# Attention decode over four layers on one core: more TensorE loops, sums folded into the heads' product, one maximum product, wo rows in two banks

## The chip, the core and the metric

The kernel runs on one core of a Trainium2 chip. The metric is the device time of one execution in microseconds (us). The engines named below are TensorE (PE, with its weight loads shown as PEld), VectorE (DVE), ScalarE (ACT), GpSimd (POOL) and SyncE (SP), which issues nearly all transfers.

## What is computed

Four layers of one-token attention over a cache, A, B, A, B, each with 32 heads of 192 numbers and 8192 cached keys and values per head. All tensors are bf16; x has 640 numbers.

```python
def _A_ref(x, k_cache, v_cache, wq, wo):
    ...
    q = (x @ wq).reshape(B, Sq, Hq, Dh).transpose(0, 2, 1, 3)
    ...
    scores = jnp.einsum("bhqd,bhkd->bhqk", q, k) * (Dh ** -0.5)
    p = _softmax(scores, axis=-1)
    o = jnp.einsum("bhqk,bhkd->bhqd", p, v)
    return o.transpose(0, 2, 1, 3).reshape(B, Sq, Hq * Dh) @ wo
...
x = A_x
x = x + _A_ref(_layernorm(x, axis=-1), A_k_cache, A_v_cache, A_wq, A_wo)
x = x + _B_ref(_layernorm(x, axis=-1), B_k_cache, B_v_cache, B_wq, B_wo)
x = x + _A_ref(_layernorm(x, axis=-1), A_k_cache, A_v_cache, A_wq, A_wo)
x = x + _B_ref(_layernorm(x, axis=-1), B_k_cache, B_v_cache, B_wq, B_wo)
```

_B_ref computes the same as _A_ref. The caches do not fit on the core, so nearly all of them is read twice.

## The kernel before

**Tiling.** Heads are taken two at a time: 16 pairs in each of 4 layers. A pair's keys lie on 128 partitions, 64 for each head, 128 keys per partition, and are handled in two halves u = 0, 1 of 64 keys (3072 KB each); so are its values. They land in `pool`, eight slots of one half each. A whole pair of keys or values is one transfer of 6144 KB into two slots, or two of 3072 KB (`whole`).

**Order.** Python lists fix the order. `steps` is the order of compute, `plan` that of the transfers; `allot` gives each transfer the slots that come free first, `released` says after which step, and `transfer` lets SP wait for the event in `freed`. SP has one queue in order: a transfer that waits for its slot holds up all behind it. Each engine's instructions are a `Queue`; `settle` drops waits that others imply, and `bank` makes users of one PSUM bank wait for the last use by other engines.

**Steps of a pair.** For pair p of layer l, `products` (step m, L693) multiplies each half of the keys by q on VectorE in place (L705), in NC cuts over the 192 numbers: two cuts of 96 in pairs 2 to 13 of layers 0, 1 and 3, four of 48 elsewhere. TensorE sums over the numbers with the identity as weights, 24 products a half of 8 numbers x 64 keys into `S`: in pairs with two cuts by `matmul_loop` (L83, a loop on TensorE with two products a turn, L95) apart from the first and last two, else written out (L725). Layer 2's pair 0 goes in quarters (`quarter`). `softmax` (step s) reduces S to scores (L785), takes the largest of each partition (L787), brings these across the partitions by two products of 64 columns (L790), reduces them to the negated maximum (L794), and lets ScalarE form the exponentials and their sums (L800). `values` (step v) sums the sums of exponentials over the partitions (L815, or L819 for the last pair) into bank TB and multiplies the exponentials with the values into O in bank group OY, in four column groups (L842), eight keys at a time, or two in a layer's last pair. `gather` (step e) takes the reciprocal of the sums (L856), picks the wanted parts of O on VectorE (L866 and L868, or L861 and L862 for the last pair), sums them by the heads' product into TB (L880, or L876), and scales them into `rows` by ScalarE (L889).

**Steps of a layer.** `q_rows` and `q_spread` (L606) form the row of all q and spread the pair's part over the partitions into bank QM (L610, copied at L572); q_spread for the next pair stands behind the second half's scores. After pairs 4, 9 and 14, `columns` (L681) turns the gathered row into columns and `project_row` (L651) multiplies 15 of them with the block of wo: for each column, two products of 320 numbers (L658) into YR, partitions 0 and 32 of one bank. `to_columns` turns the row sum into columns (L671, L675); in layer 1 that follows the second block, and the third is done in columns by `project` (L624). In layers 1 and 3 the last 5 and 7 columns of the third block are a transfer and a step of their own (wob), and the last value half comes in two quarters (vq). `busy` gives TensorE products without use to keep its clock up.

**The end.** In layer 3 the last steps are: m of pair 15, v of pair 14, s of 15, busy 16, e of 14, first half of v of 15, columns, eight columns of wo, second half of v of 15 with busy 6 ahead of its last quarter, e of 15 with busy 3, and ten columns of wo (7 in wob, 2 in wol, 1 in woe). ScalarE copies YR (L948) and SP sends it out.

Of the kernel before, what the change touches and what calls it, by code (L numbers as in the profile page):

```python
# [5 lines left out]
ALU = mybir.AluOpType  # L6
# [76 lines left out]
def matmul_loop(t, waits, out, lhsT, rows, first, count, regs, at, label, begin):  # L83

    b, width, m = t.bass, out.shape[-1] // rows.shape[1], len(regs)
    for i in range(m if begin else 0):
        t.reg_mov(regs[i], at + 2 * (first + i * width))
# [19 lines left out]
NSLOT = 8  # L107
KEPT = {0: {("k", 0)}, 1: {("v", 14), ("v", 15)}}


def build(nc, A_x, A_k, A_v, A_wq, A_wo, B_x, B_k, B_v, B_wq, B_wo, out):
# [28 lines left out]
    with ExitStack() as ctx:  # L140
# [19 lines left out]
        acc = sb("acc", [P, DH], F32)  # L160
        q_sb = [sb(f"q_sb{i}", [P, DH], BF16) for i in range(2)]
        ones = sb("ones", [P, 1], F32)
        one_b = sb("one_b", [P, 1], BF16)
        small = sb("small", [P, 82], F32)
# [7 lines left out]
        half = col(2)  # L172
        half33 = col(33)
        neghalf = col(1)
        s_sb = [sb(f"s_sb{i}", [P, J], F32) for i in range(2)]
# [3 lines left out]
        l_col = [col(2) for i in range(2)]  # L179
# [12 lines left out]
        zero = sb("zero", [P, 33], BF16)  # L192
        part = [sb(f"part{i}", [P, DC], BF16) for i in range(3)]
# [8 lines left out]
        YR = YB[0:33, 64:64 + HD]  # L202
        TB = ps("TB")
        use = {b: {} for b in ("QM", "S0", "S1", "O", "TB", "YB")}
        QMu, Ou, TBu, YBu = [(use[b],) for b in ("QM", "O", "TB", "YB")]
# [3 lines left out]
        C_ST = 64  # L209
        C_L = 72  # L210
        C_O = 128
# [15 lines left out]
        PO.op(lambda g: g.memset(zero[:], 0.0))  # L227
        mask = acc[:, 0:2 * VK].rearrange("p (h i) -> p h i", h=2)
# [9 lines left out]
        PO.op(lambda g: g.memset(half33, 0.0))  # L238
        ev_const = PO.op(lambda g: g.memset(neghalf[:], -0.5))
        DV.op(lambda v: v.tensor_reduce(pick[:], mask.rearrange("p h i -> p i h"), AX.X, ALU.add), ev_mask)  # L240
        e = DV.op(lambda v: v.tensor_reduce(half[:], mask, AX.X, ALU.add), ev_mask)
        ev_pick = DV.op(lambda v: v.tensor_copy(half33[:, 0:33:32], half[:]), e, ev_const)
# [273 lines left out]
        def sums(ev_z):  # L516
# [5 lines left out]
            e = PE.op(lambda t: t.matmul(TB[:, C_ST:C_ST + 2], lhsT=ones[:, 0:1].broadcast_to([P, P]), rhs=st[:], start=True, stop=True),  # L522
                      e, ev_const, last["stt"], bank=TBu)
            last["st"] = e
            e = DV.op(lambda v: v.tensor_scalar(mv[:], TB[:, C_ST:C_ST + 2], 1.0 / D, None, ALU.mult), e, last["rs"], bank=TBu)
# [3 lines left out]
        def layer(l, ev_z, ev_true):  # L529
# [76 lines left out]
            def q_spread(p):  # L606

                PE.wait(last["rows"], last["QB"], ev_const)
# [22 lines left out]

            def to_row():

                e = DV.op(lambda v: v.tensor_copy(z[:], x_true[:]), ev_true)
                for i in range(3):
                    e = DV.op(lambda v, i=i: v.tensor_copy(part[i][:], z[:]), e)
                    if i < 2:
                        e = DV.op(lambda v, i=i: v.tensor_tensor(z[:], z[:], part[i][:], ALU.subtract), e)
# [373 lines left out]
```

## Time and profile before

| what | value |
|---|---|
| median of 3 runs | 1980.01 us (1979.34 to 1980.67) |
| the profiled execution | 1979.76 us, of which the span is 1978.0 |
| PE, PEld busy | 1272.5 us, 129.3 us |
| DVE, ACT busy | 1198.5 us, 168.1 us |
| mean granted TensorE clock | 0.788 |
| read from HBM | 848.36 MB, 429 GB/s over the span |
| L705, products of keys and q | 837.5 us in 360 instructions |
| L95 and L77 into S, looped and held score products | 382.3 us in 1440, 426.1 us in 1564 |
| L658, wo rows | 41.1 us in 330 |

The span runs from the first to the last instruction, the time of an execution also holds what lies around it. A matmul's end is modelled, so intervals between starts say more of TensorE than its busy time. The granted clock is the share of full speed that the throttle lets TensorE have; the trace has it at 0.50 or 1.00 for some microseconds each.

### The profile page before, as it was taken

To read this page: it belongs to the slowest core of one execution; us is meant where nothing else is said; L and a number is where in the kernel's file an instruction comes from. 1 tells how busy PE (TensorE), PEld (TensorE's weight loads), DVE (VectorE), ACT (ScalarE), POOL (GpSimd) and SP (SyncE) were. 2 spreads that over 40 slices of the span, in tenths; PEclk is the share of its full clock that TensorE was granted. 3 is DMA by queue.
4 is the path that set the end of the run, shared out by engine and by line. 5 is a ranking of instruction groups with operands and counts; after the bars stand their busy time and mean duration, and the time that the engine had idled before them with its cause. 6 is when DMAs were issued, how large, how long until landed. Compare 5 with 4: busy or idle time off the path is not lost.

```text
span 1978.0 us, 13592 instructions
## 1 busy us (share of the span) xinstructions
PE 1272.5 (64%) x7742; PEld 129.3 (7%) x2599; DVE 1198.5 (61%) x812; ACT 168.1 (8%) x529; POOL 4.6 (0%) x24
## 2 busy tenths in 40 slices
PE   3566566567465666665775665666676667657558
PEld 0000000000200100000020000000002001000001
DVE  3566466467166656656755565665764665765756
ACT  0000000000000100100010000000000100000000
POOL 0000000000000000000000000000000000000000
PEclk9787777777687777787887877878787787878778
DMA  9999999999999999999999999999999999999998
GB/s 414 435 434 430 433 431 431 436 432 427 433 436 434 432 430 430 430 431 433 429 415 435 426 426 433 431 430 431 434 429 428 434 431 434 432 432 434 432 432 373
DMA packets 27093, 849.09 MB, mean 429 GB/s; under 512 B 3106, under 2 KB 3236, under 8 KB 3876
## 3 DMA queue, kind: packets, MB, share of 16 engines
q1 hardware_dynamic: 26900, 848.38, 99.7%
q8 instruction: 38, 0.62, 0.1%
q14 instruction: 11, 0.09, 0.0%
q10 hardware_dynamic: 144, 0.00, 0.0%
HBM read 848.36 MB, written 0.00 MB: 429 GB/s over the span
## 4 chain that ended last, share of the span: by engine, by line
DMA 53%; PE 29%; DVE 16%; ACT 2%; issue 1%; SPq 0%
DMA pool<-in_B_k_cache_dram 22%; DMA pool<-in_A_v_cache_dram 15%; DMA pool<-in_A_k_cache_dram 14%; DVE pool L705 11%; PE S L95 8%; PE S L77 7%; PE OY L77 5%; PE OY L842 4%; DMA pool<-in_B_v_cache_dram 2%; DVE s_sb L785 2%; PE OY L658 1%; DVE OY L866 1%; DVE acc L868 1%; ACT p_sb L800 1%; PE S L725 0%
## 5 line engine op out<-in xcount | busy, mean ns | idle before, releaser
L705 DVE TENSOR_TENSOR pool<-pool,q_sb 128x3072 bf16<-128x3072 bf16 (+1 forms) x360 | 837.5, 2392 | 147.0 <-DMA pool<-in_B_k_cache_dram 81.9
L77 PE MATMUL S<-pool,ident 128*128 128x512 bf16 x1564 | 426.1, 422 | 10.8 <-DVE pool L705 10.3
L95 PE MATMUL S<-pool,ident 128*128 x1440 | 382.3, 427 | 2.5 <-DVE pool L705 2.3
L866 DVE TENSOR_TENSOR OY<-OY,small 128x1536 f32<-128x1536 f32 x60 | 106.0, 1766 | 254.2 <-PE OY L77 254.1
L77 PE MATMUL OY<-pool,p_sb 128*16 128x512 bf16 x1920 | 206.2, 518 | 0.0
L880 PE MATMUL TB<-acc,small 128*33 128x192 f32 x120 | 44.5, 467 | 210.3 <-DVE acc L868 210.3
L785 DVE TENSOR_REDUCE s_sb<-S 128x128 f32<-128x1024 f32 x63 | 77.1, 1224 | 163.3 <-PE S L77 163.3
L842 PE MATMUL OY<-pool,p_sb 128*16 128x512 bf16 (+1 forms) x1216 | 144.2, 497 | 47.5 <-DMA pool<-in_A_v_cache_dram 43.9
L725 PE MATMUL S<-pool,ident 128*128 128x512 bf16 x36 | 21.0, 584 | 153.4 <-DVE pool L705 153.4
L572 ACT ACTIVATE q_sb<-QM 64x192 bf16<-64x192 f32 x120 | 38.9, 324 | 941.5 <-PE QM L610 940.8
L868 DVE TENSOR_REDUCE acc<-OY 128x192 f32<-128x1536 f32 x60 | 105.4, 1757 | 2.0
L889 ACT ACTIVATE rows<-TB,small 1x192 bf16<-1x192 f32 x120 | 49.4, 412 | 556.2 <-PE TB L880 554.7
L800 ACT ACTIVATE p_sb<-s_sb,small 64x128 bf16<-64x128 f32 x128 | 55.7, 435 | 170.1 <-DVE small L794 169.3
L856 DVE RECIPROCAL small<-TB 33x2 f32<-33x2 f32 x64 | 11.1, 173 | 95.0 <-PE TB L815 78.2
L790 PE MATMUL QM<-ident,m_bf 128*64 128x64 bf16 x128 | 14.1, 217 | 82.5 <-DVE m_bf L787 82.5
L815 PE MATMUL TB<-small,ones 128*33 128x2 f32 x120 | 14.5, 191 | 74.0 <-ACT p_sb L800 74.0
L742 PE MATMUL S<-pool,ident 128*128 128x512 bf16 x28 | 15.8, 563 | 58.7 <-DVE pool L705 58.7
L610 PEld LDWEIGHTS QM<-rows,one_b 1*128 1x128 bf16 x60 | 5.5, 91 | 734.4 <-issue 728.5
L842 PEld LDWEIGHTS OY<-pool,p_sb 128*16 128x16 bf16 (+1 forms) x1216 | 35.6, 108 | 199.1 <-issue 141.5
L658 PE MATMUL OY<-pool,oT 128*1 128x320 bf16 x330 | 41.1, 431 | 2.2 <-ACT oT L688 2.2
L794 DVE TENSOR_REDUCE small<-QM 128x1 f32<-128x64 f32 x64 | 14.3, 224 | 29.9 <-PE QM L790 29.9
L880 PEld LDWEIGHTS TB<-acc,small 128*33 128x33 f32 x120 | 10.1, 130 | 294.9 <-DVE acc L868 289.7
(90 smaller groups left out, 279.3 us busy)
## 6 DMA issues: line engine op xcount, KB each, us to landing
pool<-in_B_k_cache_dram SPq DMA_DIRECT2D x28, 6144.0 KB, 35.9
pool<-in_B_v_cache_dram SPq DMA_DIRECT2D x28, 6144.0 KB, 29.2
pool<-in_A_v_cache_dram SPq DMA_DIRECT2D x27, 6144.0 KB, 26.3
pool<-in_A_k_cache_dram SPq DMA_DIRECT2D x34, 3072.0 KB, 20.4
pool<-in_A_k_cache_dram SPq DMA_DIRECT2D x14, 6144.0 KB, 34.5
pool<-in_A_v_cache_dram SPq DMA_DIRECT2D x9, 3072.0 KB, 14.5
pool<-in_B_k_cache_dram SPq DMA_DIRECT2D x8, 3072.0 KB, 21.4
pool<-in_A_wo_dram SPq DMA_DIRECT2D x6, 2400.0 KB, 21.2
```

The costliest lines, as they stand in the source:

```text
L77: return t.add_instruction(mybir.InstMatmult(name=t.bass.get_next_instruction_name(), engine=mybir.EngineType.PE, ins=[t.lower_ap(rhs), t. ...
L95: t.add_instruction(mybir.InstMatmult(name=b.get_next_instruction_name(), engine=mybir.EngineType.PE, ins=[x.__replace__(regref=reg.name, ...
L572: lambda a, h=h, r=r, f=f: a.activation(q_sb[i][r, :], QM[r, h * DH:(h + 1) * DH], ACT.Copy, scale=f),
L658: e = PE.op(lambda t, i=i, h=h, f=l < 3 and n[2] == 0 and i == 0, fin=n == last_row and i == k - 1: t.matmul(YR[32 * h:32 * h + 1, :], lhs ...
L705: e = DV.op(lambda v, d0=d0: v.tensor_tensor(k3[:, :, d0:d0 + QD], kin[:, :, d0:d0 + QD], q_sb[qi][:, d0:d0 + QD].unsqueeze(1).broadcast_t ...
L785: lambda v: v.tensor_reduce(s[:], S_[:].rearrange("p (j r) -> p j r", r=R), AX.X, ALU.add),
L800: ev_p[p] = AC.op(lambda a, h=h, r=r: a.activation(p_sb[par][r, :, h], s[r, :], ACT.Exp, bias=negm[par][r, 0:1], accum_out=l_col[par][r, h ...
L842: t.matmul(o, lhsT=x, rhs=y, start=f, stop=fin) if c == 0 else
L866: e = DV.op(lambda v: v.tensor_tensor(o3, o3, pick[:, 0:VK].unsqueeze(2).broadcast_to([P, VK, DH]), ALU.mult), bank=Ou)
L868: e = DV.op(lambda v: v.tensor_reduce(acc[:], O.rearrange("p (i d) -> p d i", d=DH), AX.X, ALU.add), e, bank=Ou)
L880: e = PE.op(lambda t: t.matmul(TB[64:97, C_O:C_O + DH], lhsT=half33, rhs=acc[:], start=True, stop=True), bank=TBu)
L889: last["TO"] = last["row_written"] = AC.op(lambda a, h=h: a.activation(orow[:, o0 + h * DH:o0 + (h + 1) * DH], TB[64 + 32 * h:65 + 32 * h, ...
```

## The change

Eight edits, in one diff:

- **Cuts and loops.** Every half of keys is cut in two, and both halves of its score products run as loops. The pairs of layer and number in `FINE` are cut in 96, 48 and 48, with a loop for the first cut alone. Registers for the loops are set by an addition.
- **Sums of exponentials.** They lie beside `acc` in one tile, and the heads' product takes both: weights `heads` (ones in columns 0 to 32, the heads' masks at 64 and 96), two more moving columns. L815 is gone but for a layer's last pair. The reciprocal and the row copies, `rest`, are put off to the next call of `finish`.
- **Maximum.** One product of 128 columns; the negated maximum is reduced in two halves of the partitions.
- **Wo rows.** The two products of a column go to partition 0 of two banks, YB and YC, the second with the first one's weights. The row's copy is two instructions, one on ScalarE and one on VectorE.
- **Banks.** TB's uses move to QM; its place is YC.
- **Layer 1's third wo block** is done in rows, and `to_columns` follows it, not the second.
- **Layer 0's last pair** takes eight keys at a time, as other pairs do.
- **q_spread** for the next pair stands behind the first half's scores, and the last score product of the second half waits for the copied q.

```diff
-        t.reg_mov(regs[i], at + 2 * (first + i * width))
+        t.reg_add(regs[i], t.zero_reg, at + 2 * (first + i * width))
...
+FINE = {(1, 15), (2, 1), (2, 15), (3, 0)}
...
+        acc_l = sb("acc", [P, DH + 4], F32)
+        acc = acc_l[:, 2:2 + DH]
...
+        heads = col(97)
+        half = heads[:, 64:97:32]
...
+        l_col = [acc_l[:, i * (DH + 2):i * (DH + 2) + 2] for i in range(2)]
...
-        YR = YB[0:33, 64:64 + HD]
-        TB = ps("TB")
+        YC = ps("YC")
+        YR = [b[0:1, 64:64 + HD] for b in (YB, YC)]
...
             def q_spread(p):
 
+                finish()
                 PE.wait(last["rows"], last["QB"], ev_const)
...
+            def pair_of_rows(x, rhs, start, stop, signal):
+
+                for h in range(2):
+                    e = PE.op(lambda t, h=h: (matmul_held(t, YR[1], x, rhs(1), start, stop, 32, 0) if h else
+                                              t.matmul(YR[0], lhsT=x, rhs=rhs(0), start=start, stop=stop, skip_group_check=True)),
+                              signal=signal and h == 1, bank=YRu[h])
+                return e
...
-            last_row = ("woe", l) if l == 3 else ("wo", l, 1 if NB[l] else 2)
+            last_row = ("woe", l) if l == 3 else ("wo", l, 2)
...
-                    for h in range(2):
-                        e = PE.op(lambda t, i=i, h=h, f=l < 3 and n[2] == 0 and i == 0, fin=n == last_row and i == k - 1: t.matmul(
-                            YR[32 * h:32 * h + 1, :], lhsT=o[:, i:i + 1], rhs=t3[:, i, h * HD:(h + 1) * HD], start=f, stop=fin,
-                            skip_group_check=True), signal=(i == k - 1 and h == 1), bank=YBu)
-                last["oT"] = e
+                    e = pair_of_rows(o[:, i:i + 1], lambda h, i=i: t3[:, i, h * HD:(h + 1) * HD],
+                                     l < 3 and n[2] == 0 and i == 0, n == last_row and i == k - 1, i == k - 1)
+                last["oT"] = freed[("woa",) + n[1:]] = e
...
+            def row_copies(a, ev_y):
+
+                return (AC.op(lambda c: c.activation(a[0:1], YR[0], ACT.Copy), ev_y, bank=YBu),
+                        DV.op(lambda v: v.tensor_copy(a[32:33], YR[1]), ev_y, bank=YCu))
...
+            end_keys = VK if l == 0 else 2
+            undone = []
+
+            def finish():
+                if undone:
+                    undone.pop()()
...
-                NC = 2 if l != 2 and 2 <= p < NPAIR - 2 else 4
-                QD = DH // NC
-                for c in range(NC):
-                    d0 = c * QD
-                    e = DV.op(lambda v, d0=d0: v.tensor_tensor(
+                cuts = [DH // 2] + [DH // 4] * 2 if (l, p) in FINE else [DH // 2] * 2
+                starts = [sum(cuts[:c]) for c in range(len(cuts))]
+                for d0, QD in zip(starts, cuts):
+                    e = DV.op(lambda v, d0=d0, QD=QD: v.tensor_tensor(
...
+                    finish()
...
+                        if u == 1 and r == DH // R - 1:
+                            PE.wait(ev_q.get(p + 1))
...
+                PE.wait(chunks[0])
+                scores(0, m)
+                loop(0)
+                PE.wait(chunks[1])
+                if len(cuts) == 2:
+                    loop(1)
+                    e = scores(DH // R - m, DH // R)
+                else:
+                    scores(n, n + n // 2)
+                    PE.wait(chunks[2])
+                    e = scores(n + n // 2, DH // R)
...
+                e = PE.op(lambda t: t.matmul(QM[:, C_MX:C_MX + P], lhsT=m[:, 0:1].broadcast_to([P, P]), rhs=ident[:],
+                                             start=True, stop=True), ev_m, last["MX"], bank=QMu)
+                last["m"][par] = e
                 for h in range(2):
...
+                    r = slice(64 * h, 64 * h + 64)
+                    ev_n = DV.op(lambda v, r=r: v.tensor_reduce(negm[par][r], QM[r, C_MX + r.start:C_MX + r.stop], AX.X, ALU.max,
+                                                                negate=True), e, last["negm"][par], signal=h == 1, bank=QMu)
...
+                x = acc_l[:, 2 * par:2 * par + DH + 2]
+                cl, co = (DH, 0) if par else (0, 2)
+                last["acc"] = last["lc"][par] = e = PE.op(lambda t: t.matmul(
+                    QM[0:97, 0:DH + 2], lhsT=heads, rhs=x, start=True, stop=True), ev_p[p], bank=QMu)
+
+                def rest():
+                    ev_rl = last["rl"] = DV.op(lambda v: v.reciprocal(rl[64:97, 0:2], QM[0:33, cl:cl + 2]), e, last["TO"], bank=QMu)
...
+                undone.append(rest)
...
-                if q_ready and (n[0] in ("wq", "r") and l >= 2 or n[0] == "m" and n[3] == 1):
+                if q_ready and (n[0] in ("wq", "r") and l >= 2 or n[0] == "m" and n[3] == 0):
```

## The prediction, made before the change was run

> **What bounds the kernel now.** I read the page's queue part first, then the slices, then the chain of waits at its end, then the engines' timeline there.
>
> ```profile
> DMA  9999999999999999999999999999999999999998
> ...
> q1 hardware_dynamic: 26900, 848.38, 99.7%
> ```
>
> The cache queue holds the 16 DMA engines 99.7% of the span and no slice shows a hole: 848 MB are read as fast as they come, whatever the engines do. So inside the span an engine's gain is worth nothing, and its loss nothing while the queue keeps a transfer in hand. What counts lies behind the landing of the last key pair but one at 1924.4. The chain of waits (start, length, what) has that transfer last and compute alone behind it:
>
> ```profile
> 1882.28 42.12 DMA pool<-in_B_k_cache_dram
> ...
> 1924.42 1.77 DVE pool L705
> ...
> 1968.05 0.98 PE OY L658 x12
> ...
> 1970.27 1.08 PE S L77 x5
> ```
>
> The timeline gives its durations (start, length, engine, line, and in brackets the idle time before):
>
> ```profile
> 1924.42 13.44 DVE L705 TENSOR_TENSOR pool<-pool,q_sb 128x3072 bf16<-128x3072 bf16 x8 [1.32 <-DMA pool<-in_B_k_cache_dram]
> ...
> 1939.50 1.22 DVE L785 TENSOR_REDUCE s_sb<-S 128x128 f32<-128x1024 f32 x1 [1.64 <-PE S L77]
> ...
> 1941.36 0.23 DVE L794 TENSOR_REDUCE small<-QM 128x1 f32<-128x64 f32 x1 [0.32 <-PE QM L790]
> 1941.50 13.43 DVE L705 TENSOR_TENSOR pool<-pool,q_sb 128x3072 bf16<-128x3072 bf16 x8
> ...
> 1956.56 1.22 DVE L785 TENSOR_REDUCE s_sb<-S 128x128 f32<-128x1024 f32 x1 [1.63 <-PE S L77]
> ...
> 1959.83 0.17 DVE L856 RECIPROCAL small<-TB 33x2 f32<-33x2 f32 x1
> ...
> 1960.03 1.77 DVE L866 TENSOR_TENSOR OY<-OY,small 128x1536 f32<-128x1536 f32 x1
> ...
> 1971.29 0.82 PE L842 MATMUL OY<-pool,p_sb 128*4 128x384 bf16 x16
> ...
> 1973.95 1.11 PE L658 MATMUL OY<-pool,oT 128*1 128x320 bf16 x14
> ```
>
> L705 of pair 14, S, softmax, L705 of pair 15, S, the values of pair 14, L866 and L868, heads, columns, wo rows, the last quarter of the values, wo rows, copy, output: each starts where the one before ends. In it PE meets the last value transfer: the fifth filler product on L77 starts at 1970.97 and the values restart at 1971.29, where the transfer landed at 1971.25. At a filler's 0.216 us PE would have been free at 1971.19, so its slack there is 0.1 us. The tail is both the only place where the change can cost, and a place with no cover.
>
> **The change, part by part.** The profiled execution took 1979.76 us, span 1978.0; the median of the runs shown is 1980.01, 0.25 more.
>
> *Score cuts.* Pairs 0, 1, 14, 15 and layer 2 had four cuts a half; now all have two, but for the four in FINE, with three. Layer 3's pairs 14 and 15 are not in FINE. Two-cut pairs of layer 3 read so in the same view:
>
> ```profile
> 1789.43 1.22 DVE L785 TENSOR_REDUCE s_sb<-S 128x128 f32<-128x1024 f32 x1 [3.38 <-PE S L77]
> ...
> 1866.29 13.16 DVE L705 TENSOR_TENSOR pool<-pool,q_sb 128x6144 bf16<-128x6144 bf16 x4 [1.24 <-DMA pool<-in_B_k_cache_dram]
> 1882.29 1.23 DVE L785 TENSOR_REDUCE s_sb<-S 128x128 f32<-128x1024 f32 x1 [2.84 <-PE S L77]
> ...
> 1912.11 1.22 DVE L785 TENSOR_REDUCE s_sb<-S 128x128 f32<-128x1024 f32 x1 [3.59 <-PE S L77]
> ```
>
> VectorE needs 13.16 instead of 13.44 and 13.43: -0.55 over both pairs. But twelve products wait for the last cut, not six, and the idle time before L785 is 2.84 five times and 3.38, 3.64, 3.59 in the last eight two-cut pairs, mean 3.10 (the long ones where the granted clock was still 0.50 well into the pair), against 1.64 and 1.63 here. That is 2 x (3.10 - 1.635) = +2.93; bounds +2.41 (2.84 twice) and +4.01 (3.64 twice).
>
> *Maximum.* One product of 128 columns replaces two of 64 (L790, 0.22 together): 0. The reduction L794 becomes two of half the partitions, 0.23 each, by the row: +0.25 after pair 14, with its 0.02 hop. After pair 15 it takes the place of the reciprocal L856 (0.20 with its hop), which moves: +0.05. Bounds: 0 if a half costs half, 0.5.
>
> *Sums in the heads' product.* L815 (0.16 on the chain, 1956.53 to 1956.68) goes: -0.16. The heads' product gets 97 weight columns instead of 33 and 194 moving columns instead of 192; L880 took 0.53 for its two passes, a load of 64 columns (L819) 0.13 instead of 0.11: +0.05. The reciprocal now follows this product, and the two L889 copies follow it: +0.20 (0.17 and a hop). For pair 13 the deferred reciprocal slips in between L705's first cut and the second of pair 14: +0.20. Sum +0.29; bounds 0 and 0.5.
>
> *Wo rows.* Each row's two products went to PSUM partitions 0 and 32; now both go to partition 0, in two banks, with one weight load. At granted clock 1.0, single starts on L658 in the tail stand in twos, 2 to 4 ns apart, and 135 ns from pair to pair: 320 columns are streamed once for both. Products on one position stand apart by their full stream: 216 ns for 512 columns on L77, so 135 for 320. A row then takes 270 instead of 135, and the saved load, which PEld runs beside the products, gives nothing back. Eight rows before the wait: +1.08, less the 0.10 of slack; ten after it: +1.35. Bounds: 0 if two banks overlap, +2.43.
>
> The Trainium skill ("TensorE: Matmul & The Clock Gate", section "Why this matters for your kernels") says that small-M matmuls run at once when their outputs lie in different column groups of partitions, and puts three such at 2.38 times, not 3. Taken as 79% of the ideal, an estimate from that page, two would gain 1.59 and the rows would lose 18 x 80 ns = 1.4 instead of 2.43, the whole sum being 1.0 lower. The trace's 2 to 4 ns between starts speaks for the full factor, so I keep 2.43.
>
> *Copy at the end.* L948 (0.43 for 33 partitions) becomes one row on ScalarE and one on VectorE, side by side; L889 takes 0.41 for one row: 0.
>
> *Loops.* They save PE instructions. The instruction queue holds 0.1% of 16 engines: 38 fetches of 16 KB, about 1.05 us of one engine each, so 40/16 = 2.5 us of the stream in all. About 20 score instructions in each of 23 pairs, the 165 second loads of rows, and L815 are roughly 900 of the 10,341 that the page counts on PE and PEld: 9% of 2.5, -0.2, as the stream reaches 1924.4 that much sooner. Bounds 0 and -0.5.
>
> *Under cover.* The same edits delay earlier stages: a wo block there runs mostly at clock 0.50, 267 ns a row (L658, 1173.74 to 1177.70), so +2.0 to +3.7 each; the score end +1.3; in layer 0 the last pair's gather takes L866 and L868 (3.5) instead of L861 and L862 (0.9), +2.6; in layer 1 to_columns (L671, L675, 2.5) moves from the second wo block behind the third, and L624's columns become rows: about +4, less 1.6 that PE idles for the value landing at 1008.78. All of this delays slot releases and so SP's next transfers, which queue in order behind one wait. The cover is the transfer still in flight: between issue and the landing ahead of it lie mostly 8 to 25 us, least 4.2 (value half issued at 1177.74, behind a wo block, landing ahead 1181.94), then 4.5 (1054.47), 5.4 (1328.34) and 5.5 (852.85, 1542.60). The first transfer needed 1.0 from issue to its first packet. Worst: 4.2 - 2.3 = 1.9, still over 1.0. Cost 0; without cover 1 to 3 us at each. The q product moves from behind the second half's scores to behind the first half's; it issues no transfer and passes no DMA queue, and the new wait for q before the last score product, with the maximum and the values queued behind it, ends about 6 us early. The uses of TB move into QM's bank and wait on one another; those on the chain are counted above.
>
> *Sum.* -0.55 + 2.93 + 0.25 + 0.05 - 0.16 + 0.05 + 0.20 + 0.20 + 1.08 - 0.10 + 1.35 - 0.20 = +5.1. 1979.76 + 5.1 + 0.25 = **1985.1 us**, +0.26%. One cannot tell less than 0.2%, about 4 us, from no change here. With the bounds of scores and rows alone it runs from 1982.2 to 1986.2.
>
> **Rivals.**
> (1) The queue runs dry: if the wo blocks after 1173 and 1324 stay at clock 0.50 throughout (+3.7) and the score end adds its 1.3, the 4.2 and 5.4 go under 1.0 and the stream loses 1 to 2 us at each: 1988. For: these blocks start at 0.50. Against: the clock goes to 1.00 at 1177.37 and 1327.55, and v's release there does not wait for scores.
> (2) Other side: the two rows overlap though on one position, since they write two banks. Then the 2.43 falls out: 1982.7, within 0.2%, not slower. It decides once a row takes under about 200 ns at clock 1.0. For: nothing but the two banks. Against: L77's 216 ns, held weights.
> (3) The wider cuts do not delay the end of S (PE warm throughout): 1985.1 - 2.9 = 1982.2. Against: all eight rows.
> (4) The loops free the stream by more than I think: even all fetches gone are 2.5, against 5.3 lost. Faster only if most of the tail's costs fall too.
>
> **How the numbers follow.** Forecast 0.66, (1) 0.12, (2) 0.12, (3) 0.05, (4) 0.05. Slower by over 0.2%: (1), and of the forecast all but its low end: 0.70. Same: that end 0.08, (2), (3): 0.25. Faster: 0.05. The range reaches from (2) and (3), 1982.0, to (1), 1988.5.
>
> **What would show it.** The key landing before pair 14 still near 1924; idle before the S reductions of pairs 14 and 15 near 3 instead of 1.6; rows 270 ns apart in the tail and the last ten taking 2.7 instead of 1.4; PE, no longer the landing, setting the restart of the last values, near 1975. A DMA share under 0.9 in some slice between 1050 and 1560 would show (1); row starts 135 apart (2). I am wrong if the landing near 1924 moves by over 2 us, or the span from it to the end does not grow.

## The result, and the profile after

| | before | changed |
|---|---|---|
| median (lowest to highest, runs) | 1980.03 us (1979.28 to 1980.67, 6) | 1994.9 us (1990.64 to 1999.18, 6) |
| ratio, with its 95% interval | | 1.0075 (1.0062 to 1.0088) |
| the profiled execution | 1979.76 us, span 1978.0 | 1999.18 us, span 1997.4 |
| landing of the key pair ahead of pair 14, layer 3 | 1924.40 | 1934.92 |
| from that landing to the issue of the output | 51.57 | 60.47 |

The change makes the kernel 14.9 us slower by the medians; 5.1 was predicted. The last two rows split the difference of the profiled executions: the stream arrives 10.52 later and the tail takes 8.90 more, together 19.42, which is 1999.18 - 1979.76. The profiled execution is the longest of the six, so this split is that of a long one; the profile of e14_fill3, further down, the same instructions up to the tail, splits into 7.64 and 6.33.

The rates of the kernel before by slice, then of the changed kernel the slices of the DMA engines and of the rate, and its cache queue:

```profile
GB/s 414 435 434 430 433 431 431 436 432 427 433 436 434 432 430 430 430 431 433 429 415 435 426 426 433 431 430 431 434 429 428 434 431 434 432 432 434 432 432 373
```

```profile
DMA  9999999999999999999999999999999999999997
GB/s 412 434 432 433 428 437 429 436 429 427 435 436 429 435 429 434 432 430 435 416 371 413 430 414 439 425 412 433 432 433 425 434 430 437 436 423 435 437 428 304
...
q1 hardware_dynamic: 26900, 848.38, 99.0%
```

The digits hide what the rates show: the 21st slice (999 to 1048 us) moved 371 GB/s, where the kernel before moved 415. The views by window, first of the kernel before, then of the changed one (window, length, busy time of PE, PEld, DVE, ACT and POOL, granted clock, share of the DMA engines, GB/s):

```profile
1020.00:1030.00 10.00, 9.77 (x59) 0.46 (x9) 10.00 (x8) 0.00 (x0) 0.00 (x0) 1.00 0.99 402
1180.00:1190.00 10.00, 8.58 (x38) 0.00 (x0) 8.20 (x5) 0.00 (x0) 0.00 (x0) 1.00 1.01 433
1340.00:1350.00 10.00, 6.72 (x61) 0.83 (x21) 2.53 (x6) 1.63 (x6) 0.00 (x0) 0.83 1.00 430
1962.43:1965.85 3.42, 1.93 (x26) 0.69 (x26) 1.16 (x1) 0.82 (x2) 0.00 (x0) 1.00 1.00 424
```

```profile
1020.00:1030.00 10.00, 7.98 (x59) 2.28 (x35) 5.80 (x13) 0.83 (x2) 0.55 (x1) 0.83 0.78 278
1180.00:1190.00 10.00, 9.21 (x57) 2.61 (x31) 6.96 (x3) 0.62 (x3) 0.00 (x0) 0.75 0.88 351
1340.00:1350.00 10.00, 9.57 (x48) 0.53 (x6) 9.08 (x3) 0.65 (x2) 0.00 (x0) 1.00 0.82 327
1976.79:1980.21 3.42, 1.60 (x23) 0.83 (x26) 1.13 (x3) 0.83 (x2) 0.00 (x0) 1.00 1.01 426
```

In the first three windows the DMA engines stood idle for 2.2, 1.2 and 1.8 us where before they were full: the hand-over from layer 1 to layer 2, and the places behind the first two wo blocks of layer 2. There the queue runs dry. Idle time is not all of it: from 975 to 1075 us the share is 0.95 where it was 1.00, and the rate 385 GB/s where it was 420. Of some 8 us of stream lost in these 100, about 5 are idle time; in the rest the engines are busy and move less, and why no run shows. The fourth line of each belongs to the tail and is read below.

The timeline of the tail in the changed kernel (start, length, engine, line, and in brackets the idle time before):

```profile
1934.95 3.36 DVE L727 TENSOR_TENSOR pool<-pool,q_sb 128x6144 bf16<-128x6144 bf16 x1 [1.30 <-DMA pool<-in_B_k_cache_dram]
...
1938.53 9.90 DVE L727 TENSOR_TENSOR pool<-pool,q_sb 128x6144 bf16<-128x6144 bf16 x3
...
1951.41 1.23 DVE L805 TENSOR_REDUCE s_sb<-S 128x128 f32<-128x1024 f32 x1 [2.99 <-PE S L77]
...
1953.28 0.46 DVE L814 TENSOR_REDUCE small<-QM 64x1 f32<-64x64 f32 x2 [0.32 <-PE QM L809]
...
1970.68 1.23 DVE L805 TENSOR_REDUCE s_sb<-S 128x128 f32<-128x1024 f32 x1 [3.75 <-PE S L77]
...
1979.35 0.28 PE L836 MATMUL QM<-acc,small 128*64 128x1 f32 x4 [1.14 <-ACT rows L912]
...
1979.56 2.15 PE L860 MATMUL OY<-pool,p_sb 128*4 128x384 bf16 x32
...
1983.47 0.47 PE L642 MATMUL OY<-pool,oT 128*1 128x320 bf16 x1
1983.73 0.47 PE L77 MATMUL YC<-pool,oT 128*1 128x320 bf16 x1
...
1984.00 0.47 PE L642 MATMUL OY<-pool,oT 128*1 128x320 bf16 x1
...
1989.27 0.82 PE L860 MATMUL OY<-pool,p_sb 128*4 128x384 bf16 x16
...
1992.44 0.30 PE L642 MATMUL OY<-pool,oT 128*1 128x320 bf16 x1
1992.58 0.30 PE L77 MATMUL YC<-pool,oT 128*1 128x320 bf16 x1
...
1992.71 0.30 PE L642 MATMUL OY<-pool,oT 128*1 128x320 bf16 x1
...
1994.81 0.43 ACT L682 ACTIVATE pool<-OY 1x320 bf16<-1x320 f32 x1 [2.54 <-PE YC L77]
1994.81 0.48 DVE L683 CAST pool<-YC 1x320 bf16<-1x320 f32 x1 [3.80 <-PE YC L77]
```

S of pairs 14 and 15 ends 2.99 and 3.75 us behind the last cut instead of 1.64 and 1.63. A wo row's first product (L642) stands 270 ns from the next one at the end, as forecast, but 530 ns at 1983.47: the granted clock is 0.50 from 1980.21 to 1987.04. That follows the window shown above in which TensorE was busy for 1.60 of 3.42 us; the window of before with the same work had 1.93, and kept its clock.

### The profile page after: what moved, and what is told of

It reads as the page before. It is cut to its first block, busy times and chain, and to the rows that moved or that the text cites. A ratio compares the mean times of both kernels' runs of the same rounds, so it can differ in the third digit from the quotient of the medians.

```text
span 1997.4 us, 13922 instructions
## 1 busy us (share of the span) xinstructions
PE 1296.3 (65%) x7513; PEld 134.8 (7%) x2201; DVE 1213.7 (61%) x779; ACT 168.3 (8%) x529; POOL 4.6 (0%) x25
## 4 chain that ended last, share of the span: by engine, by line
DMA 44%; PE 34%; DVE 19%; ACT 2%; issue 1%; SPq 0%
DMA pool<-in_B_k_cache_dram 17%; DMA pool<-in_A_v_cache_dram 15%; PE S L95 14%; DMA pool<-in_A_k_cache_dram 13%; DVE pool L727 12%; PE OY L77 6%; PE OY L860 4%; PE S L77 3%; DVE s_sb L805 2%; DVE OY L884 2%; DVE acc L886 2%; PE OY L642 1%; PE YC L77 1%; ACT p_sb L820 1%; PE S L744 1%
## 5 line engine op out<-in xcount | busy, mean ns | idle before, releaser
L727 DVE TENSOR_TENSOR pool<-pool,q_sb 128x6144 bf16<-128x6144 bf16 (+1 forms) x260 | 834.7, 3256 | 102.3 <-DMA pool<-in_B_k_cache_dram 52.8
L95 PE MATMUL S<-pool,ident 128*128 x2440 | 642.1, 423 | 7.9 <-DVE pool L727 6.9
L744 PE MATMUL S<-pool,ident 128*128 128x512 bf16 x121 | 59.0, 488 | 207.8 <-DVE pool L727 207.8
L904 PE MATMUL QM<-acc,small 128*97 128x194 f32 x120 | 54.6, 556 | 211.5 <-DVE acc L886 210.6
L77 PE MATMUL S<-pool,ident 128*128 128x512 bf16 x507 | 166.2, 410 | 0.2 <-DVE pool L777 0.2
L912 ACT ACTIVATE rows<-QM,small 1x192 bf16<-1x192 f32 x120 | 49.5, 413 | 703.2 <-DVE small L908 701.7
L809 PE MATMUL QM<-ident,m_bf 128*128 128x128 bf16 x64 | 14.7, 229 | 98.2 <-DVE m_bf L807 98.2
L642 PE MATMUL OY<-pool,oT 128*1 128x320 bf16 x175 | 61.9, 369 | 2.5 <-ACT oT L705 2.5
L77 PE MATMUL YC<-pool,oT 128*1 128x320 bf16 x175 | 61.0, 364 | 0.0
L814 DVE TENSOR_REDUCE small<-QM 64x1 f32<-64x64 f32 x128 | 28.4, 222 | 26.5 <-PE QM L809 25.6
L904 PEld LDWEIGHTS QM<-acc,small 128*97 128x97 f32 x120 | 22.4, 243 | 293.8 <-DVE acc L886 292.8
```

The lines of the kernel that those rows point to most:

```text
L77: return t.add_instruction(mybir.InstMatmult(name=t.bass.get_next_instruction_name(), engine=mybir.EngineType.PE, ins=[t.lower_ap(rhs), t. ...
L95: t.add_instruction(mybir.InstMatmult(name=b.get_next_instruction_name(), engine=mybir.EngineType.PE, ins=[x.__replace__(regref=reg.name, ...
L642: t.matmul(YR[0], lhsT=x, rhs=rhs(0), start=start, stop=stop, skip_group_check=True)),
L727: e = DV.op(lambda v, d0=d0, QD=QD: v.tensor_tensor(k3[:, :, d0:d0 + QD], kin[:, :, d0:d0 + QD], q_sb[qi][:, d0:d0 + QD].unsqueeze(1).broa ...
L744: t.matmul(S[:, :], lhsT=ident[:], rhs=x, start=f, stop=fin)),
L904: last["acc"] = last["lc"][par] = e = PE.op(lambda t: t.matmul(QM[0:97, 0:DH + 2], lhsT=heads, rhs=x, start=True, stop=True), ev_p[p], ban ...
```

## The experiments

Products without use, where an experiment adds them, write what nothing reads. To each median belongs one of the kernel before from the same chip: 1979.69 for e1 to e4, 1979.78 for e5, e6, e7 and e9, 1980.11 for e8 and e11 to e13, 1980.18 for e10 and e14. "Stream" and "tail" are the two numbers of the table above for the experiment's profiled execution, as differences to before.

### One part undone

**e1_groups**: wo rows back in two column groups of one bank.

```diff
-        YR = [b[0:1, 64:64 + HD] for b in (YB, YC)]
+        YR = [YB[32 * h:32 * h + 1, 64:64 + HD] for h in range(2)]
...
-                    e = PE.op(lambda t, h=h: (matmul_held(t, YR[1], x, rhs(1), start, stop, 32, 0) if h else
...
+                    e = PE.op(lambda t, h=h: t.matmul(YR[h], lhsT=x, rhs=rhs(h), start=start, stop=stop, skip_group_check=True),
```

> The changed kernel (median 1994.9) with the two products of a wo row back in two column groups of one bank, each with its own weight load; all else as changed. Theory 1 (late slot releases starve the transfer queue at the layer 1 to 2 hand-over and behind layer 2's wo blocks, and the tail grows by the same rows): rows cost 2.3 us of the hand-over's 7.1, all of the losses near 1187 and 1341 (1.2 and 1.6) and in the tail 3.1 before the last values and 1.4 after them; 1984 to 1987 us. Theory 2 (the wider score cuts do most of it, the rows only their 2.4 at full clock): 1991 to 1993. Theory 3 (the throttle alone, tipped by the reciprocal behind the heads' product): 1992 to 1995, with the granted clock at 0.50 in the tail's wo block.

Measured 1988.46 (1985.43 to 1989.72), ratio 1.0041 (1.0027 to 1.0055); stream +1.65, tail +3.76. Here and in e4 both copies of the row read one bank and run one after the other (1980.41 and 1980.87), so that the output is issued 0.97 behind the start of the first and not 0.46 as in e9: 0.5 of the tail belongs to that.

**e2_cuts**: four cuts a half and written-out scores again in pairs 0, 1, 14, 15 and in layer 2.

```diff
-                cuts = [DH // 2] + [DH // 4] * 2 if (l, p) in FINE else [DH // 2] * 2
+                old = l == 2 or not 2 <= p < NPAIR - 2
+                cuts = [DH // 4] * 4 if old else [DH // 2] + [DH // 4] * 2 if (l, p) in FINE else [DH // 2] * 2
...
+                if old:
+                    for c in range(4):
+                        PE.wait(chunks[c])
+                        e = scores(c * (n // 2), (c + 1) * (n // 2))
```

> The changed kernel with four score cuts, written out, where the kernel before had them (layer 2, and pairs 0, 1, 14, 15 of the others); all else as changed. Theory 1: tail 3.2 us shorter (S of pairs 14 and 15 in time), hand-over from layer 1 to 2 2.6 earlier; 1987 to 1990 us. Theory 2: 1984 to 1986. Theory 3: 1991 to 1995.

Measured 1987.39 (1985.41 to 1989.79), ratio 1.0038 (1.0024 to 1.0052); stream +4.06, tail +3.58.

**e3_l1cols**: layer 1's third wo block in columns, to_columns behind the second.

```diff
-            last_row = ("woe", l) if l == 3 else ("wo", l, 2)
+            last_row = ("woe", l) if l == 3 else ("wo", l, 1 if NB[l] else 2)
...
-                    project_row(n, slot[place[n]][:, 0:k * D], oT[:, 0:k], last["oTw"])
+                    e = (project_row if l == 3 or n[2] < 2 or NB[l] == 0 else project)(
+                        n, slot[place[n]][:, 0:k * D], oT[:, 0:k], last["oTw"])
```

> The changed kernel with layer 1's third wo block in columns and the turning of the row sum behind the second block, as before; all else as changed. Theory 1: the hand-over from layer 1 to 2 comes some 4.5 us earlier and most of its 8.3 us of lost transfer time are back, the tail is unchanged; 1986 to 1989 us. Theories 2 and 3: 1992 to 1995.

Measured 1999.16 (1997.39 to 2001.39), ratio 1.0101 (1.0084 to 1.0118); stream +8.96, tail +8.68: a miss. Its VectorE has the reason:

```profile
838.77 0.16 DVE L908 RECIPROCAL small<-QM 33x2 f32<-33x2 f32 x1 [0.90 <-PE QM L904]
847.30 0.48 DVE L683 COPY pool<-YC 1x320 f32<-1x320 f32 x1 [8.37 <-PE YC L77]
847.82 13.16 DVE L727 TENSOR_TENSOR pool<-pool,q_sb 128x6144 bf16<-128x6144 bf16 x4
```

The change puts one of the two row copies on VectorE. Behind the second block that copy stands in VectorE's queue ahead of pair 10's products, waits 8.37 us for the rows, and the products wait behind it. The next key transfer was issued at 858.30, when the queue had been dry for 0.7 us, and the DMA engines idled 4.0 us around it. The run thus tells nothing of the moved block; e10 repeats it without that copy.

**e4_all3**: the three undone together.

> The three undone together: rows in two groups, four cuts, layer 1's third block in columns. What is left of the change is the sums in the heads' product, the maximum in one product, the shared bank, the earlier q and layer 0's last pair. Theories 1 and 2: 1979.5 to 1981 us, with no loss of transfer time between 1000 and 1070 and a tail within 1 us of the one before. Theory 3: 1983 or more, the throttle still at 0.50 in the tail.

Measured 1982.64 (1980.94 to 1984.26), ratio 1.0014 (1.0004 to 1.0023); stream -0.11, tail +1.51. VectorE's copy is still there, and the issue near 856 was 2.1 ahead of the dry queue. With e1 and e2 it shows that neither rows nor cuts carry the loss alone. In the changed kernel that copy comes behind layer 1's third block: it waits 8.02 us there too (to 1012.11), but nothing waits behind it, since VectorE's next work waits for TensorE until 1017.41.

### One part kept

In these the row's copies are all on ScalarE.

**e9_base**: all three undone; what stays of the change is the sums, the maximum, the shared bank, the earlier q and layer 0's last pair. The further loops are undone with the cuts: L95 has 1440 products as before, and 2440 in the changed kernel.

> As e4_all3, but with the row sum copied by one instruction on ScalarE, as before, and not by ScalarE and VectorE one after the other. In e4_all3 VectorE's copy stood in its queue behind pair 9's gather and ahead of pair 10's products, so that these began at 844.92 instead of 836.52, and 1.2 us of transfers were lost there. Theory 1: that loss goes, and 0.5 of the tail: 1980.5 to 1981.5 us. If VectorE's copy is not the cause: 1982 to 1983.

Measured 1980.46 (1979.4 to 1984.16), ratio 1.0005 (0.9996 to 1.0015); stream -1.07, tail +0.64. Its S reductions wait as before:

```profile
1938.66 1.23 DVE L809 TENSOR_REDUCE s_sb<-S 128x128 f32<-128x1024 f32 x1 [1.54 <-PE S L77]
...
1956.00 1.23 DVE L809 TENSOR_REDUCE s_sb<-S 128x128 f32<-128x1024 f32 x1 [1.54 <-PE S L77]
```

**e6_rows**: e9 with the rows in two banks.

> Of rows, cuts and layer 1's block only the rows as changed: four cuts as before, layer 1's third block in columns and the turning of the row sum behind the second one, the row sum copied by ScalarE alone (two copies, one for each bank; VectorE does not wait for it). Theory 1: the tail pays 2.4 at full clock or 4.5 at half, layer 2's blocks near 1180 and 1335 and layer 1's second block near 855 lose 1 to 3 each; 1987 to 1992 us. Theory 2: 1983 to 1985.

Measured 1987.35 (1986.67 to 1988.53), ratio 1.0039 (1.0025 to 1.0054); stream +3.94, tail +3.50. Leads (from a transfer's issue to the landing of the one ahead) of 2.1, 1.1 and 1.7 us at 855, 1181 and 1334. Its two row copies at the end stand one behind the other on ScalarE:

```profile
1982.51 0.43 ACT L682 ACTIVATE pool<-OY 1x320 bf16<-1x320 f32 x1 [2.54 <-PE YC L77]
1982.96 0.43 ACT L683 ACTIVATE pool<-YC 1x320 bf16<-1x320 f32 x1
```

The second one, 0.44 of the tail, is in e10 too, but not in the changed kernel.

**e7_cuts**: e9 with the wide cuts.

> Of rows, cuts and layer 1's block only the cuts as changed: rows in two groups, layer 1's block as before with one copy on ScalarE. Theory 1: tail +3.2, hand-over 2.6 later, which its cover just takes; 1984 to 1986 us. Theory 2: 1988 or more.

Measured 1986.33 (1985.15 to 1988.31), ratio 1.0032 (1.0019 to 1.0045); stream +5.31, tail +3.25. Leads of 3.25 and 2.44 at 855 and 992. From 975 to 1075 us the DMA share is 0.99 and the rate 409 GB/s (1.00 and 421 in e9): most of what is lost there is not idle time.

**e8_l1**: e9 with the moved block of layer 1.

> The changed kernel with the rows back in two column groups of one bank (one copy by ScalarE) and the four cuts a half back where they were; layer 1's third wo block stays in rows with to_columns behind it. With the three parts undone the time is 1980.5. Theory (at the hand-over from layer 1 to layer 2 the leads are 5 to 6 us, and the moved block alone takes 1 to 2 of them): 1980.5 to 1982, no lead there under 3.5. Rival (the moved block is what starves the queue): 1983 or more, leads of 2 or less at issues 1021 to 1031.

Measured 1982.81 (1980.38 to 1984.51), ratio 1.0011 (1.0002 to 1.0020); stream -0.92, no lead under 3.9, tail +3.30. The moved block alone starves nothing; the rival falls. In its tail the clock was 0.50 from 1965.51 to 1972.34, in e9's it stayed at 1.00, though the work is the same. The gap of TensorE behind pair 14's gather fell whole into one of the throttle's windows of 3.41 us (1962.10 to 1965.51, TensorE busy for 1.59 of it); in e9 it lies across two (busy for 2.73 and 2.27). So 2.7 of its tail is a matter of where the windows lie, and its median's 2.3 over e9 may be no more than that.

Less the kernel before of the same chip, e9 stands at +0.7, rows alone at +7.6, cuts at +6.6, the block at +2.7. So rows bring 6.9, cuts 5.9, the block 2.0; all three 14.8 on top of 0.7, that is 15.5, 0.4 of it e6's second copy, and the changed kernel has 14.9. They add up within the noise, and taking rows or cuts out of the whole gives the like: 6.1 (e1, 8.8 left) and 7.2 (e2, 7.7 left).

### What makes the stream late

**e12_late2** and **e13_late3**: e9 with seven TensorE products without use ahead of the first two wo blocks of layer 2, or of layer 3. The added lines are e12's; e13 has `l == 3`.

```diff
+                if l == 2 and n[0] == "wo" and n[2] < 2:
+                    busy(7)
                 PE.wait(ev_o, need(n), last["YB"])
```

> The kernel with the three parts undone (median 1980.5), plus seven TensorE products without use ahead of the first two wo blocks of layer 2 (after pairs 4 and 9). Nothing else changes: no row, cut or copy. Behind each of these blocks a value transfer is issued 4.0 us before the landing ahead of it (issues 1176.42 and 1329.05). Seven such products last at most 3.0 us, some 0.3 of it in an idle stretch, and TensorE's clock may come up sooner: the release is 1 to 2.7 late, the lead 1.3 to 3. Theory (the queue's engines go idle once a transfer is issued less than about 3.5 us before the landing ahead of it): 0.5 to 2.2 us of idle time at each place and 1981.5 to 1984.5. Rival (the cover lasts down to a lead of about 1.0, as predicted): no idle time at either place, 1980.5.

> The same seven products without use ahead of the first two wo blocks of layer 3 instead, where transfers are issued 13 us and more before the landing ahead of them. Theory and rival of the previous run both expect no idle time there and 1980.5. A third reading (a delay of TensorE costs its length wherever it stands, or the clock is spent) would give 1982 to 1984.

Measured 1982.54 (1980.24 to 1985.52), ratio 1.0011 (1.0002 to 1.0020), and 1980.15 (1979.40 to 1983.25), ratio 1.0002 (0.9993 to 1.0011). By the medians the same delay costs some 2.4 us in layer 2 and nothing in layer 3, where every lead is 13 us or more. The size is less sure than the sign: of the 4.4 us that the stream of e12's profile is later than e9's, 2.6 are there by 1059, where both are one program (at 855 it had a lead of 3.2 and idled 0.9). Windows of e9, then of e12, at the two delays:

```profile
1180.00:1190.00 10.00, 8.45 (x37) 0.19 (x2) 7.98 (x5) 0.65 (x2) 0.00 (x0) 1.00 1.00 428
1335.00:1345.00 10.00, 6.16 (x29) 0.24 (x6) 6.87 (x7) 1.24 (x5) 0.00 (x0) 1.00 1.01 430
```

```profile
1180.00:1190.00 10.00, 9.53 (x45) 0.28 (x3) 8.48 (x6) 0.65 (x2) 0.00 (x0) 1.00 0.94 380
1335.00:1345.00 10.00, 9.47 (x44) 0.19 (x2) 7.73 (x6) 0.65 (x2) 0.00 (x0) 1.00 0.93 396
```

With leads of 4.04 and 4.07 the engines stayed full; with 3.74 and 2.31 they lost 0.6 and 0.7 us in these windows. The cover wears out below some 4, not at 1.0. All 16 profiles of this study say the same (leads of SP's issues between 25 and 1900 us, and the idle time of the DMA engines from the issue to 4 us behind the landing ahead of it, worked out from the traces):

| lead, us | issues | idle: median | lowest to highest |
|---|---|---|---|
| under 1.5 | 5 | 1.13 | 0.56 to 1.16 |
| 1.5 to 2.5 | 18 | 0.90 | 0.56 to 1.23 |
| 2.5 to 3.5 | 14 | 0.54 | 0.09 to 1.44 |
| 3.5 to 4.0 | 17 | 0.09 | 0 to 0.48 |
| 4.0 to 5.0 | 92 | 0.05 or less | 0 to 0.95 |

**e10_l1act**: e3 with both row copies on ScalarE.

```diff
-                return (AC.op(lambda c: c.activation(a[0:1], YR[0], ACT.Copy), ev_y, bank=YBu),
-                        DV.op(lambda v: v.tensor_copy(a[32:33], YR[1]), ev_y, bank=YCu))
+                AC.op(lambda c: c.activation(a[0:1], YR[0], ACT.Copy), ev_y, bank=YBu)
+                return (AC.op(lambda c: c.activation(a[32:33], YR[1], ACT.Copy), ev_y, bank=YCu),)
```

> The changed kernel with layer 1's third wo block in columns again and to_columns behind the second block, as before, and both row copies on ScalarE, not one of them on VectorE. It is the run without VectorE's copy that the first run of this part should have been. If VectorE's copy held up pair 10's products there, the issue near 856 keeps a lead of about 2 (it had -0.7) and its idle falls from 4.0 to 1.5. Theory (moved block and hand-over are one of several late releases): the hand-over's 8 us of lost stream shrink to 0 to 3, the losses behind layer 2's wo blocks stay, 1989 to 1993. Rival (rows and cuts alone make the loss, the moved block counts for nothing): 1993.3, the sum of the effects of rows and cuts measured alone, or more.

Measured 1994.45 (1993.16 to 2000.13), ratio 1.0077 (1.0064 to 1.0091), against 1994.9 with the block moved; stream +10.35, tail +8.72. VectorE's products of pair 10 start at 837.73 instead of 847.82, and the lead near 857 is 1.3 instead of -0.7, so the copy was e3's trouble. But the theory falls and the rival holds: without the moved block the loss is as large. It stands elsewhere (windows of e10):

```profile
850.00:860.00 10.00, 10.00 (x41) 0.28 (x3) 0.90 (x1) 0.65 (x2) 0.00 (x0) 0.86 0.74 290
1020.00:1030.00 10.00, 8.62 (x49) 1.07 (x13) 7.49 (x9) 0.83 (x2) 0.55 (x1) 0.83 1.01 394
1180.00:1190.00 10.00, 10.00 (x47) 1.34 (x12) 9.36 (x3) 0.00 (x0) 0.00 (x0) 0.81 0.77 312
```

2.6 us near 855 and 2.3 near 1185, none at the start of the hand-over. Landings of the same transfers, later than in the kernel before, in us:

| landing before | 872.88 | 1058.95 | 1181.94 | 1333.76 | 1493.07 | 1924.40 |
|---|---|---|---|---|---|---|
| changed | -0.3 | +7.5 | +7.7 | +9.3 | +10.5 | +10.5 |
| e14_fill3 | +0.6 | +4.7 | +5.3 | +6.0 | +7.6 | +7.6 |
| e10_l1act | +1.3 | +4.0 | +4.8 | +6.8 | +9.1 | +10.4 |
| e6_rows | -0.1 | -0.1 | -0.2 | +2.3 | +3.9 | +3.9 |
| e9_base | -0.2 | -1.0 | -1.5 | -0.6 | -0.9 | -1.1 |

Nearly all is lost between 850 and 1500, where ten leads of before were 4.2 to 6.6 us, and hardly any where they are longer.

### The clock in the tail

**e5_fill** and **e14_fill3**: the changed kernel with five products without use behind the heads' product of pair 14, in layers 1 and 3, or in layer 3 alone. The edit is e5's; e14 has `l == 3` in place of `NB[l]`.

```diff
                     QM[0:97, 0:DH + 2], lhsT=heads, rhs=x, start=True, stop=True), ev_p[p], bank=QMu)
+                if p == NPAIR - 2 and NB[l]:
+                    busy(5)
```

> The changed kernel with five more filler products on TensorE behind the heads' product of the last pair but one in layers 1 and 3, where TensorE waits 1.1 us for the reciprocal and the row copies. Theory 3 in its present form (that wait tips the throttle to 0.50 for the next two windows, which doubles the first eight or ten wo rows of the tail and of the hand-over): granted clock 1.00 through both, tail 2.5 to 3.5 us shorter, hand-over 1 to 2 earlier; 1989 to 1992 us. If the clock is not tipped by that wait: 1994 to 1996.

Measured 1992.48 (1991.69 to 1992.87), ratio 1.0064 (1.0048 to 1.0081); stream +6.13, tail +5.81.

> The changed kernel with five products without use behind the heads' product of pair 14 in layer 3 alone. Up to there it is the changed kernel instruction for instruction, so its hand-over from layer 1 to 2 is a second look at that of the profiled execution, which lost 8.35 us. Theory: the size of that loss varies with the clock in the stretch from execution to execution, so 3 to 9 us lost here; the tail, without a stretch at half clock behind pair 14's gather, takes 57.4 us instead of 60.5; median 1991 to 1993.5. Rival (the loss at the hand-over is fixed at 8.35 and the fills in layer 1 of the earlier run took 5 of it away): 8.35 lost again here and a median of 1994 or more, against 1992.5 with the fills in both layers.

Measured 1993.62 (1991.91 to 1997.38), ratio 1.0069 (1.0055 to 1.0082); stream +7.64, tail +6.33. The tail of e14, where the clock stays at 1.00:

```profile
1976.75 1.47 PE L860 MATMUL OY<-pool,p_sb 128*4 128x384 bf16 x32
...
1979.51 0.30 PE L642 MATMUL OY<-pool,oT 128*1 128x320 bf16 x1 [0.28 <-ACT oT L705]
1979.78 0.30 PE L642 MATMUL OY<-pool,oT 128*1 128x320 bf16 x1
```

The first 32 products of the values take 1.47 instead of 2.15, a row 270 ns instead of 530, and the tail is 2.57 shorter (3.09 in e5). The stretch at half clock cost that much. In the changed kernel, e3, e8 and e10 the window that fell on the gap behind pair 14's gather had 1.59 or 1.60 busy, and the clock fell in each; here, with the products without use, it had 2.67. Up to the tail e14 issues what the changed kernel issues, yet its stream is 2.9 less late, nearly all of it by 1059: the loss at the hand-over is not a fixed 8, and the changed kernel's executions differ by more than that (1990.64 to 1999.18). The median gains 1.3, less than the profiles; that would fit executions whose windows lie as e9's and that do not fall into half clock, but only profiled ones show their clock by time.

### A way to speed the rows up

**e11_four**: the kernel before with a row in four products of 160 numbers on four column groups.

```diff
-                    for h in range(2):
+                    for h in range(4):
...
-                            YR[32 * h:32 * h + 1, :], lhsT=o[:, i:i + 1], rhs=t3[:, i, h * HD:(h + 1) * HD], start=f, stop=fin,
+                            YR[32 * h:32 * h + 1, :], lhsT=o[:, i:i + 1], rhs=t3[:, i, h * HQ:(h + 1) * HQ], start=f, stop=fin,
```

> The kernel before with each wo row as four products of 160 numbers in four column groups (partitions 0, 32, 64, 96 of one bank) instead of two of 320. If column groups overlap fully, a row takes 67 ns instead of 135 at clock 1.0: the last ten rows save 0.7 us, the first eight 0.5 of which only 0.1 counts before the value landing takes over, so 1979.0 to 1979.4. If issuing four products with their loads takes as long as the streams (about 35 ns each), no change, 1979.8. If loads of weights delay it, 1980 or more. Releases in layers 2 and 3 come 1 to 2 us earlier, which saves nothing where the queue is already full.

Measured 1979.80 (1979.20 to 1981.06), ratio 0.9998 (0.9989 to 1.0007): no difference that can be told. Its TensorE in the tail:

```profile
1968.06 0.72 PE L659 MATMUL OY<-pool,oT 128*1 128x160 bf16 x32 [0.28 <-ACT oT L689]
...
1971.15 0.82 PE L843 MATMUL OY<-pool,p_sb 128*4 128x384 bf16 x16 [0.31 <-DMA pool<-in_B_v_cache_dram]
...
1973.83 0.66 PE L659 MATMUL OY<-pool,oT 128*1 128x160 bf16 x28
1974.72 0.55 PE L659 MATMUL OY<-pool,oTl 128*1 128x160 bf16 x12 [0.23 <-DMA pool<-in_B_wo_dram]
```

A row takes some 70 ns instead of 135, but both gains end in a wait for a landing: the last values at 1971.15, the last wo rows at 1974.72. Rows were no longer what the end waits for.

## Why the prediction was wrong, step by step

**What bounds the kernel.** That the tail has no cover held. That ahead of it an engine's loss is worth nothing did not: between 850 and 1500 ten transfers of the kernel before were issued only 4.2 to 6.6 us ahead of a dry queue, and about 4 are needed. By the prediction's own sign it is wrong: the landing near 1924 moved by 10.5.

**Under cover, the step that failed.** It costed all delays ahead of the tail at 0, because the worst lead, 1.9 by its own sum, was "still over 1.0". For the wo blocks of layer 2 that lead was right: the two issues behind them had 2.03 and 1.94 (at the hand-over it was less: 1.00, 1.32 and 1.52). The 1.0 was wrong. It was the time from the first issue to the first packet on an idle queue, and a busy queue needs more: between 1.5 and 2.5 us of lead, 18 issues of 18 lost 0.56 to 1.23. In place of 0 stand 7.6 to 10.5 us in the profiles (rows 5.0 of it by e6 less e9; cuts 2.7 by e1 and 6.4 by e7, each against e9, the one with the moved block and VectorE's copy, the other without). Nor was the hand-over a sum of its own "+4 less 1.6": undoing the block and VectorE's copy (e10) moves the loss elsewhere, and leaves the total. The reason is open; it would go with compute, not the stream, setting the pace from 850 to 1350, so that what one place doesn't lose the next does. Nor is it all idle time: in the changed kernel's hand-over that is some 5 of 8 us, in e7 less.

**Rival (1)** had this mechanism, with 1 to 2 us at each of two wo blocks, which is what the windows show there, 1.2 and 1.8. It got 0.12 because of the same 1.0, and lacked the hand-over. Its sign, a slice under 0.9, did not come, since 2 us are 4% of a slice of 50.

**Score cuts.** +2.93 - 0.55 = 2.38 forecast; cuts alone lengthen the tail by 2.61 (e7 less e9). In the changed kernel the two idle times are 2.99 and 3.75, +3.47 over before instead of +2.93, within the bound of 4.01. Rival (3) falls.

**Maximum and sums.** Their terms make +0.59; without rows, cuts and block the tail is +0.64, +0.61 and +0.61 (e9, e12, e13). Right, and the best-sized part. TensorE's wait for ScalarE's copies before the last sums, 1.14 where it was 0.94 (L819), is the +0.20.

**Wo rows.** 270 ns a row at clock 1.00, as forecast; rival (2) falls, two banks do not overlap. Alone they lengthen the tail by 2.86 (e6 less e9), of which 0.44 is e6's second copy at the end: 2.42, where 2.33 was forecast. The Trainium skill ("TensorE: Matmul & The Clock Gate", section "Why this matters for your kernels") gives three small products in separate column groups a gain of 2.38; here two groups gained the full 2 (135 against 270) and four nearly 4 (70), so the measurement decides for the full factor.

**Half clock in the tail** was not in the sum: the rows were priced at clock 1.00 because those of before ran so. In the profiled execution a window falls on the gap behind pair 14's gather, 1.60 busy where before had 1.93, and the 6.83 us behind it cost 2.6 to 3.1. How the windows lie is no part of the change, and e8 shows the same with the old rows and cuts; but a gap this long should have been in the sum as a risk of 3 us. Without that stretch the tail is +5.8 and +6.3 (e5, e14) against +5.3 forecast; the parts measured alone, 0.6, 2.6 and 2.4 with 0.1 for the copies, make 5.7.

**Copy at the end.** 0.43 and 0.48 side by side, against 0.43. The output is issued 0.58 behind their start instead of 0.45: +0.13, not 0, but small.

**Loops.** -0.2 forecast, bound -0.5. No run sizes the term. The fetches fall from 38 to 33 in the changed kernel, at 1.05 us of one of 16 engines each some 0.3; but at the landing at 872.88 it is 0.3 earlier and e14, the same instructions up to there, 0.6 later. The stream of e9, e13 and e8 is 1.07, 0.97 and 0.92 earlier, without the further loops; in e9 and e8 most of it, 0.8 and 0.7, comes between the landings at 872.88 and 1058.95, and which of the other edits brings it no run shows.

## What to carry to other kernels

A queue that is full on every slice may still be a few microseconds from dry: before costing a delay at nothing, list for every transfer the time from its issue to the landing ahead of it, and find in the kernel's own profiles the lead at which idle time begins, not the start-up time of the first transfer. Undoing one of several late releases may only move the loss to the next place, so parts are sized alone against a base, not one at a time out of the whole. A gap in which TensorE merely waits, here 1.8 of 3.41 us, can halve its clock for the work behind it, so a sum over a tail needs the clock of the new tail, not of the old one.

## What was not expected of the hardware

- **The clock falls without idleness.** In the changed kernel's profile the clock fell from 1.00 to 0.50 119 times. Counted back from each fall in windows of 3.41 us, the last window had TensorE busy for 0 to 49% in 116 cases (80 or 81% in the other three), and the 214 windows that kept the clock all had 41% or more. The Trainium skill (the page named above, section "What's actually happening") lets the clock fall after an idle window of about 3.4 us; the length agrees, and that the windows run free of the program is what e8 and e9 look like, but here being a little more than half idle was enough.
- **The lead that a queue needs**: 3.5 to 4 us between issue and the landing ahead of it, for transfers of mostly 3 and 6 MB (the table above).
- **Four column groups** run one row in some 70 ns, two in 135, one in 270, at full clock.
